# Order of loads on the GpSimd queue, the rows of the last two groups over three queues, and early tables for the second spectral layer

## The chip, the cores and the metric

The kernel runs on one core of one Trainium2 chip. The time of a run is the device time of one execution in microseconds; the time of a kernel is the median of its runs. The core has five instruction queues that work side by side and wait for each other through semaphores: PE (matrix multiplication), DVE (vector), ACT (scalar and activation functions), POOL (GpSimd) and SP (here it only issues transfers). Each works its instructions in the order in which they were written. Transfers are issued from SP, ACT and POOL.

## What is computed

Four layers, one after the other, on x of 2048 rows and 1024 columns in bfloat16. A is a spectral layer, B a dense one:

```python
def _A_ref(x, w_r, w_i):
    X = rfft2(x.astype(float32))
    X = X * (w_r + 1j * w_i)
    return irfft2(X, s=(S, D)).astype(bfloat16)

def _B_ref(x, w1, b1, w2):
    h = einsum("bsd,df->bsf", x, w1) + b1
    sp = log1p(exp(-abs(h))) + where(h > 0, h, 0)
    return einsum("bsf,fd->bsd", h * tanh(sp), w2)

x = x + _A_ref(_layernorm(x), w_r, w_i)
x = x + _B_ref(_layernorm(x), w1, b1, w2)
x = x + _A_ref(_layernorm(x), w_r, w_i)
x = x + _B_ref(_layernorm(x), w1, b1, w2)
```

D is 1024, S is 2048 and F, the width of h, is 3584.

## The kernel before

A small planner in Python writes the program. Each buffer has a record of who wrote and read it last; an instruction that is added to a queue gets the waits that this record asks for, and stands in its queue at the place where the Python code adds it. So the order of the code is the order of each queue. x stays in SBUF all the time as 16 tiles of 128 rows (XS).

**Spectral layer** (`layer_A`, called with li 0 and 1). The transform over 2048 rows and 1024 columns is done as matrix products with tables of sines and cosines. It has these parts:

- `first_scales` (li 0 alone) finds the mean and the scale of each row on DVE and ACT. `scaled(j)` (L540) then multiplies the table M0 with the scale of the rows of one column: eight products of 128 x 128 for each j, on DVE (L549) and ACT (L546). So the scale comes in through the table, and x needn't be normalized itself. For li 1 the dense layer has written normalized rows, and the plain table M is used.
- `s1` (L552) multiplies XR, which holds x with its rows turned, with these tables: 16 groups j of eight matmuls (L564). Group j is copied out of PSUM by DVE if j is even (L572) and by ACT if it is odd (L570). For li 0, `scaled(0)` to `scaled(3)` come first, and `scaled(j + 4)` follows group j.
- Then come 12 steps (L775) in which eight groups g of frequencies are worked through, each at several stages at once: `s2` of group step (L625), `filter_bins` of the same group (li 0 alone: the filter's reversed half by matmuls on PE, L818, and copies on POOL, L826 and L829), `s3` of group step - 1 (L663 to L666, then the product with the filter on DVE, L674 to L681), `i1` of group step - 3 (L692), `i2` of group step - 4 (L713 and L731) in two halves, each copied to the buffer U by DVE (L739) or ACT (L741). `u_turn` then turns U's rows into UT, the input of the last transform.
- `u_turn(g, half)` (L743): the eight rows of the first half go to UT one by one, each a transfer of 32 KB issued by SP. The second half of groups 0 to 6 goes with one store to DRAM (u_scratch, by SP) and one read back into UT, issued by POOL, which waits for the store. The last group's 16 rows go one by one over SP, POOL and ACT.
- At the end of a step POOL issues what later steps need: `load_tabs` (the table FT for s3), `load_w` (the filter: the raw w_r and w_i for li 0, which filter_bins works up, and for li 1 the worked-up filter that the dense layer has kept in DRAM, w_scratch), `load_btabs` (the table BT for i1). The first ones are issued ahead of s1 (L759 to L763). FT and BT have three buffers each, U three.
- `constants` (L390, li 0 alone, called between those first loads and s1): SP loads four tables and the bias of the dense layer, and POOL casts the bias to float32 (L399).

All transfers go through one helper, so they carry the line L242 (the bias L241); the line of an instruction that issues one doesn't tell which it is, the names of what it writes and reads do.

**Dense layer** (`layer_B`, called after each spectral layer). `i4` (L859, L865) does the last transform from UT and adds to x; it needs all of UT. Then x is normalized, transposed (L896) and multiplied with W1 (`mm1`, L914) and W2 (`mm2`, L932). W1 is streamed by SP through four buffers, whose first four loads are issued at the end of layer_A (L797 to L799); W2's 28 loads follow on SP. In the first dense layer, `keep_filter` (L835) works up the filter for the second spectral layer with its own reversal table (JT2), raw filter and work buffers, and stores it to w_scratch. Tiles of x that are finished are normalized at once and stored by SP; POOL reads them back turned into XR (`xr_load`, after `open_xr`). The last of them, tile 15, goes straight from SBUF to XR in eight rows, issued by SP and ACT in turn (`xr_direct`, L492).

The buffers WT of the second layer's filter lie where W1's four buffers are.

Of the kernel before, what the change touches and what calls it, by code (L numbers as in the profile page):

```python
# [6 lines left out]
ALU = mybir.AluOpType  # L7
P = 128
# [166 lines left out]
class KB:  # L175
# [364 lines left out]
    def scaled(self, j):  # L540
        rt = self.RT
        rc = rt.ap.rearrange("p a b -> p (a b)")
        for q in range(8):
            n = 8 * j + q
            if q % 3 == 2:
                self.op(self.act, lambda e, n=n: e.activation(self.MN.ap[:, n, :], self.M0.ap, ACT.Copy, scale=rc[:, n:n + 1]),  # L546
                        reads=[rt.res, self.M0.res], parts=[self.r_mn[j]])
            else:
                self.op(self.dve, lambda e, n=n: e.tensor_scalar(self.MN.ap[:, n, :], self.M0.ap, rc[:, n:n + 1], None, op0=ALU.mult),  # L549
                        reads=[rt.res, self.M0.res], parts=[self.r_mn[j]])  # L550

    def s1(self, li):  # L552
# [22 lines left out]
        for r in ([self.MN.res, self.M0.res] + self.r_xr if not li else []):  # L575
            r.r(self.pe, self.pe.count)
            self.XR.res.r(self.pe, self.pe.count)

    def layer_A(self, li):
# [3 lines left out]
        K = 1024  # L583
        o = self.o
        pe, dve, act, sp, pool = self.pe, self.dve, self.act, self.sp, self.pool
        ring = lambda name, n, size, shape: [self.alloc(f"{name}{i}", o[name] + size * i, shape) for i in range(n)]
        WT = ring("WT", 8, 2 * K, [2, 512])
        FT = ring("FT", 3, 1536, [2, 384])
        BT = ring("BT", 3, 1536, [2, 384])
        if li == 0:  # L590
            WR = ring("WR", 2, 4 * K, [2, 2, 512])
        FD, BD = self.FD, self.BD
        SIG = 2.0 / (self.S * self.D)

        def load_tabs(g):
            self.dma(pool, FT[g % 3].ap, self.con["FT"][g], f"ft{g % 3}", writes=[FT[g % 3].res])

        def load_btabs(g):
            self.dma(pool, BT[g % 3].ap, self.con["BT"][g], f"bt{g % 3}", writes=[BT[g % 3].res])

        def load_w(g):
            if li == 0:
                self.load_wr(WR[g % 2], g)
                return
            pair = WT[2 * g % 8:2 * g % 8 + 2]
            ap = self.ARENA[:, (o["WT"] + 2 * g % 8 * 2 * K) // 2:(o["WT"] + 2 * g % 8 * 2 * K) // 2 + 2 * K]
            self.dma(pool, ap.rearrange("p (a b c) -> p a b c", a=2, b=2), self.w_d[g], f"wt{g % 4}", reads=[self.r_wd[g]],
                     writes=[w.res for w in pair])

        def filter_bins(g):  # L610
            ps, banks, _ = self.pair()
            self.filter_bins(g, ps, banks, WR[g % 2], WT[2 * g % 8:2 * g % 8 + 2], self.JT, self.r_jt, pool)

        def zslot(g, i):
            return Z[(2 * g + i) % 6]
# [85 lines left out]
        def i2(g, half):  # L701
# [38 lines left out]
            else:  # L740
                self.op(act, lambda e: e.activation(dst, ps, ACT.Copy), reads=banks, parts=[u.res])  # L741

        def u_turn(g, half):  # L743
# [20 lines left out]
        if li == 0:  # L764
# [70 lines left out]
    def keep_filter(self, g):  # L835

        o = self.o
        if g == 0:
            jt = self.alloc("JT2", o["JT2"], [4 * P])
            self.dma(self.pool, jt.ap, self.con["JT"], "jt2", writes=[jt.res])  # L840
            self.kf = (jt, self.alloc("WR2", o["WR2"], [2, 2, 512]),
                       [self.alloc(f"WS{i}", o["WT2"] + 2048 * i, [2, 512]) for i in range(2)])
            self.load_wr(self.kf[1], 0)
        jt, wr, ws = self.kf
        self.filter_bins(g, self.PS[:, 6:8, :].rearrange("p a b -> p (a b)"), self.r_bank[6:8], wr, ws, jt.ap, jt.res, self.dve)
        ap = self.ARENA[:, o["WT2"] // 2:o["WT2"] // 2 + 2048].rearrange("p (a b c) -> p a b c", a=2, b=2)
# [21 lines left out]
            self.op(self.act, lambda e: e.activation(dst, src, ACT.Copy), reads=rb, parts=[staged.res])  # L868


    def load_w1(self):
        n = self.w1_next
        self.w1_next += 1
        fg = n % 14
        b = self.w1_buf[n % 4]
        self.dma(self.sp, b.ap, self.w1.rearrange("(db dp) f -> dp db f", dp=P)[:, :, fg * 256:(fg + 1) * 256], f"w1_{n % 4}",
                 writes=[b.res])

    def layer_B(self, li, last):
        pe, dve, act, sp, pool = self.pe, self.dve, self.act, self.sp, self.pool  # L880
# [107 lines left out]
        for c in range(2):  # L988
            off = self.ob[f"AT{c}"]
# [92 lines left out]
```

## Time and profile before

| | |
|---|---|
| median of 3 runs | 1183.19 us (1181.63 to 1184.5) |
| profiled execution | 1183.94 us |
| span of its instructions | 1182.1 us |
| mean granted clock of TensorE | 0.938 |
| busy: PE, DVE, ACT, POOL | 1000.5, 383.3, 335.4, 112.7 us |

Stages of the profiled execution, from the chain of waits in order of time: the first spectral layer from the start to 182.87 us, where the first `i4` begins; the dense layer to 617.3; the second spectral layer to 758.75; the second dense layer to the end.

How to read it: a group's row has the line, the engine, the operation, what it writes and reads, the number of instructions, busy time and mean duration, then the idle time before them and what ended it. A row of a timeline has start and duration, then the same; a number in brackets is how long the engine had been idle, and what it waited for. In the names, c_ft and c_bt are the tables FT and BT in DRAM, in_A_w_r and in_A_w_i the raw filter, ARENA is the part of SBUF in which most buffers lie, so that ARENA<-ARENA as a transfer is a row of U on its way to UT, or a row of tile 15 on its way to XR. SPq, ACTq and POOLq are the queues in which transfers are issued.

### The profile page before, as it was taken

How to read it: one execution, taken by the hardware profiler on the slowest of the kernel's cores; microseconds unless marked ns; L12 is line 12 of the kernel's file. 1: busy time of each engine (PE TensorE's matmuls, PEld its weight loads, DVE VectorE, ACT ScalarE, POOL GpSimd, SP SyncE). 2: the span in 40 equal slices, each digit the busy share in tenths (PEclk: the TensorE clock that was granted, in tenths of full speed). 3: DMA queues.
4: the chain of work that ended last, by engine and by line, in shares of the span. 5: the costliest groups of instructions: out<-in, count | busy, mean ns of one | idle time of the engine just before them, and what ended most of it. 6: DMA issues, size and time to landing. Idle time of an engine off the chain costs nothing.

```text
span 1182.1 us, 14518 instructions
## 1 busy us (share of the span) xinstructions
PE 1000.5 (85%) x6090; PEld 529.5 (45%) x6185; DVE 383.3 (32%) x843; ACT 335.4 (28%) x466; POOL 112.7 (10%) x155
## 2 busy tenths in 40 slices
PE   1776725999999999999985775279999999999998
PEld 0555514444444444444434543244444444444443
DVE  7796406360143501104344841264301210000111
ACT  6645513434100044420004744143330002442000
POOL 1254210000000012100330111100000000000000
PEclk9988865999999999999997977689999999999999
DMA  9624473254300045400683354804451001220000
GB/s 279 134 81 118 94 116 81 72 161 143 107 27 19 21 130 180 143 1 19 86 124 86 109 122 87 142 2 143 143 161 35 19 26 46 72 72 1 27 18 27
DMA packets 128735, 102.49 MB, mean 87 GB/s; under 512 B 48192, under 2 KB 105792, under 8 KB 128672
## 3 DMA queue, kind: packets, MB, share of 16 engines
q1 hardware_dynamic: 114976, 69.86, 21.9%
q0 software_dynamic: 11392, 31.19, 11.6%
q10 hardware_dynamic: 2304, 0.53, 0.4%
q8 instruction: 49, 0.80, 0.3%
q14 instruction: 14, 0.11, 0.0%
HBM read 80.45 MB, written 15.99 MB: 82 GB/s over the span
## 4 chain that ended last, share of the span: by engine, by line
PE 68%; DVE 13%; DMA 10%; ACT 2%; issue 2%; SPq 2%; POOL 2%; ACTq 0%; POOLq 0%; DVEq 0%
PE PS L932 33%; PE PS L914 28%; DMA ARENA<-in_A_w_i_dram 3%; DMA u_scratch<-ARENA 2%; DMA ARENA<-ARENA 2%; DVE BN L431 2%; SPq L242 2%; DMA ARENA<-c_bt 1%; POOL ARENA L242 1%; DVE ARENA L572 1%; PE PS L896 1%; DVE ARENA L549 1%; PE PS L818 1%; DVE XS L865 1%; PE PS L692 1%
## 5 line engine op out<-in xcount | busy, mean ns | idle before, releaser
L914 PE MATMUL PS<-ARENA 128*128 128x512 bf16 x1750 | 388.4, 381 | 4.4 <-DVE ARENA L901 2.2
L932 PE MATMUL PS<-ARENA 128*128 128x512 bf16 x1754 | 387.4, 379 | 2.0
L918 ACT ACTIVATE ARENA<-PS,B 128x512 bf16<-128x512 f32 x224 | 153.6, 687 | 436.5 <-PE PS L914 436.5
L914 PEld LDWEIGHTS PS<-ARENA 128*128 128x128 bf16 x1792 | 175.3, 98 | 211.1 <-issue 3.3
L932 PEld LDWEIGHTS PS<-ARENA 128*128 128x128 bf16 x1792 | 174.7, 98 | 207.7
L937 DVE TENSOR_TENSOR XS<-PS,XS 128x512 bf16<-128x512 f32 x64 | 44.3, 692 | 500.6 <-PE PS L932 500.6
L431 DVE BATCH_NORM_STATS2 BN<-XS 128x6 f32<-128x512 bf16 x108 | 69.6, 674 | 7.4 <-DMA XS<-in_A_x_dram 6.2
L859 PE MATMUL PS<-MT,ARENA 128*128 128x32 bf16 (+1 forms) x768 | 24.4, 188 | 52.5 <-DMA ARENA<-ARENA 44.2
L865 DVE TENSOR_TENSOR XS<-PS,XS 128x512 bf16<-128x512 f32 (+1 forms) x40 | 29.1, 790 | 101.2 <-PE PS L859 101.2
L692 PE MATMUL PS<-ARENA 128*128 128x256 bf16 x256 | 38.9, 302 | 22.1 <-DMA ARENA<-c_bt 21.0
L570 ACT ACTIVATE ARENA<-PS 128x1024 bf16<-128x1024 f32 x16 | 16.2, 1022 | 120.6 <-PE PS L564 120.1
L859 PEld LDWEIGHTS PS<-MT,ARENA 128*128 128x128 bf16 x768 | 22.8, 101 | 56.0 <-issue 48.9
L670 ACT ACTIVATE ARENA<-PS 128x1024 bf16<-128x1024 f32 x32 | 32.7, 1023 | 46.0 <-PE PS L666 46.0
L692 PEld LDWEIGHTS PS<-ARENA 128*128 128x128 bf16 x256 | 27.1, 108 | 35.2 <-issue 21.0
L699 ACT ACTIVATE ARENA<-PS 128x1024 bf16<-128x1024 f32 x32 | 32.7, 1021 | 30.0 <-PE PS L692 30.0
L674 DVE TENSOR_TENSOR ARENA<-ARENA 128x1024 bf16<-128x1024 bf16 x32 | 24.5, 766 | 46.7 <-ACT ARENA L670 46.5
L412 ACT ACTIVATE ARENA<-XS 128x1024 bf16<-128x1024 bf16 x20 | 21.1, 1056 | 64.5 <-DVE XS L865 53.5
L625 PE MATMUL PS<-FD,ARENA 128*128 128x256 bf16 (+1 forms) x312 | 36.9, 273 | 2.6 <-DVE ARENA L572 2.4
L818 PE MATMUL PS<-ARENA 128*128 128x64 bf16 x192 | 24.8, 293 | 11.8 <-DMA ARENA<-in_A_w_i_dram 8.9
L713 PE MATMUL PS<-ARENA,BD 128*128 128x256 bf16 x192 | 30.9, 307 | 3.0 <-DVE ARENA L739 2.6
L625 PEld LDWEIGHTS PS<-FD,ARENA 128*128 128x128 bf16 x312 | 28.6, 106 | 9.7 <-DVE ARENA L572 2.9
L896 PE MATMUL PS<-IDENT,ARENA 128*128 128x128 bf16 x256 | 23.1, 252 | 9.5 <-DVE ARENA L474 7.8
(71 smaller groups left out, 622.9 us busy)
## 6 DMA issues: line engine op xcount, KB each, us to landing
ARENA<-in_B_w_dram SPq DMA_DIRECT2D x56, 512.0 KB, 3.9
ARENA<-in_B_w_dram SPq DMA_DIRECT2D x56, 256.0 KB, 4.2
XS<-in_A_x_dram SPq DMA_DIRECT2D x4, 1024.0 KB, 8.7
ARENA<-in_A_x_dram SPq DMA_DIRECT2D x32, 128.0 KB, 3.1
ARENA<-in_A_w_r_dram POOLq DMA_DIRECT2D x16, 256.0 KB, 4.2
ARENA<-in_A_w_i_dram POOLq DMA_DIRECT2D x16, 256.0 KB, 4.6
ARENA<-ARENA SPq DMA_DIRECT2D x128, 32.0 KB, 3.2
w_scratch<-ARENA POOLq DMA_DIRECT2D x8, 512.0 KB, 3.0
```

The lines of the kernel that those rows point to most:

```text
L242: return eng.dma_start(out_ap, in_ap).then_inc(ds.sem, 16)
L431: self.op(self.dve, lambda e: e.bn_stats(self.BN[:, j, 6 * h:6 * h + 6], self.XS[:, j, 512 * h:512 * h + 512]), reads=[self.r_xs[j]], part ...
L625: fns.append(lambda e: e.matmul(dst, at(r), FD[:, t:t + dst.shape[-1] * 2], start=start, stop=stop))
L692: fns.append(lambda e, c=c, part=part: e.matmul(ps[:, c * 256:(c + 1) * 256], yk.ap[:, part, c * P:(c + 1) * P], t[:, (128, 0)[part]:(384, ...
L818: fns.append(lambda e, col=col, j=(j0 + c) * P, mov=mov: e.matmul(ps[:, col:col + 64], jt[:, j:j + P], mov, start=True, stop=True))
L859: fns.append(lambda e, l=l: e.matmul(ps[:, w * l:w * l + w], self.UT.ap[:, u0 + l, :], self.MT[:, 8 * lo:8 * lo + w], start=True, stop=True))
L865: self.op(self.dve, lambda e: e.tensor_tensor(xs, src, xs, ALU.add), reads=rb, parts=self.r_xs[lo:lo + nb])
L896: fns.append(lambda e, db=db: e.transpose(PSb[:, bank, db * P:(db + 1) * P], xn.ap[:, db * P:(db + 1) * P], self.IDENT[:]))
L914: fns.append(lambda e, db=db, bank=bank, fl=fl: e.matmul(PS[:, bank, :], wb.ap[:, db, fl * P:(fl + 1) * P], x.ap[:, db, :], start=(db == 0 ...
L918: self.op(act, lambda e, bank=bank, ft=ft: e.activation(at.ap[:, ft, :], PS[:, bank, :], ACT.Mish, bias=self.B1[:, ft:ft + 1]), reads=[sel ...
L932: fns.append(lambda e, i=i, ft=ft: e.matmul(PS[:, bank, :], at.ap[:, ft, t * P:(t + 1) * P], W2[ft].ap[:, h * 512:(h + 1) * 512], start=(i ...
L937: self.op(dve, lambda e: e.tensor_tensor(xs, PS[:, bank, :], xs, ALU.add), reads=[self.r_bank[bank]], writes=[self.r_xs[j]])
```

## The change

`xr_direct` issues its eight rows from SP, ACT and POOL in turn. In `scaled`, of each eight products ACT takes the second and the sixth (before: the third and the sixth), POOL the third, fifth and eighth, and DVE the other three (before: six).

The first loads of a spectral layer move into a function `open_tables`. For li 0 it is called where the loads were before, ahead of `constants` and `s1`. For li 1 it is called in the first dense layer, after the `mm2` of the third quarter of the rows and ahead of the `xr_load`s.

Within the steps, the read back of a group's second half is no longer issued in `u_turn` but at the end of the next step, behind the loads of that step (`u_back`). Only groups 0 to 5 still go through DRAM. Group 6 goes row by row: its first half from SP, its second from POOL. Group 7's first half goes from SP and POOL by turns, its second from ACT (five rows) and SP (three).

W1's first four loads and the load of the reversal table JT2 now wait until UT has been written.

```diff
-            prog = self.act if h % 2 else self.sp
+            prog = (self.sp, self.act, self.pool)[h % 3]
...
-            if q % 3 == 2:
+            if q % 4 == 1:
                 self.op(self.act, lambda e, n=n: e.activation(...))
             else:
-                self.op(self.dve, lambda e, n=n: e.tensor_scalar(...))
+                self.op(self.pool if q % 8 in (2, 4, 7) else self.dve, lambda e, n=n: e.tensor_scalar(...))
...
+    def open_tables(self, li):
+        self.li = li
+        self.WT = self.ring("WT", 8, 2048, [2, 512])
+        self.FTr = self.ring("FT", 3, 1536, [2, 384])
+        self.BTr = self.ring("BT", 3, 1536, [2, 384])
+        if li == 0:
+            self.WR = self.ring("WR", 2, 4096, [2, 2, 512])
+        for g in range(2 if li == 0 else 4):
+            self.load_w(g)
+        for g in range(2):
+            self.load_tabs(g)
+            self.load_btabs(g)
...
     def layer_A(self, li):
         if li == 0:
             self.junk = self.alloc("JUNK", self.o["JUNK"], [self.D])
             self.first_scales()
         if li == 0:
+            self.open_tables(0)
+            self.constants()
...
-            if half and g < 7:
+            if half and g < 6:
                 self.dma(sp, self.u_d[g], u.ap[:, 8:16, :], f"uw{g % 3}", reads=[u.res], writes=[self.r_ud[g]])
-                self.dma(pool, self.UT.ap[64 + g:P:8, :, :], self.u_d[g].rearrange("l r n -> r l n"), f"um{g % 3}",
-                         reads=[self.r_ud[g]], parts=[self.UT.res])
                 return
+            order = {6: (sp, pool), 7: ((sp, pool, sp, pool, sp, pool, sp, pool), (act, sp, act, act, sp, act, sp, act))}
+            who = order[g][half] if g in order else sp
             for i in range(8):
-                r = 8 * half + i
-                prog = sp
-                if g == 7:
-                    prog = (sp, sp, pool, sp)[i % 4] if half == 0 else (act, act, pool, act)[i % 4]
-                self.dma(prog, self.UT.ap[r * 8 + g:r * 8 + g + 1, :, :], u.ap[:, r, :], f"u{prog.name}{g % 3}",
-                         reads=[u.res], parts=[self.UT.res])
-
-        for g in range(2 if li == 0 else 4):
-            load_w(g)
-        for g in range(2):
-            load_tabs(g)
-            load_btabs(g)
-        if li == 0:
-            self.constants()
+                row(who[i] if isinstance(who, tuple) else who, g, 8 * half + i)
+
+        def u_back(g):
+            self.dma(pool, self.UT.ap[64 + g:P:8, :, :], self.u_d[g].rearrange("l r n -> r l n"), f"um{g % 3}",
+                     reads=[self.r_ud[g]], parts=[self.UT.res])
         self.s1(li)
...
             if 0 <= g4 < 8 and g4 + 2 < 8:
                 load_btabs(g4 + 2)
+            if 0 <= g5 - 1 < 6:
+                u_back(g5 - 1)
...
-            self.load_w1()
+            self.load_w1(after=[self.UT.res])
...
-            self.dma(self.pool, jt.ap, self.con["JT"], "jt2", writes=[jt.res])
+            self.dma(self.pool, jt.ap, self.con["JT"], "jt2", reads=[self.UT.res], writes=[jt.res])
...
         if not last:
             self.open_xr()
+            self.open_tables(1)
             for j in range(12):
                 self.xr_load(j)
```

More of the change, by code (lines that the diff above doesn't have):

```diff
@@ L548, in scaled @@
             else:
[L549 removed]
+                self.op(self.pool if q % 8 in (2, 4, 7) else self.dve, lambda e, n=n: e.tensor_scalar(self.MN.ap[:, n, :], self.M0.ap, rc[:, n:n + 1], None, op0=ALU.mult),
                         reads=[rt.res, self.M0.res], parts=[self.r_mn[j]])
@@ L577, in s1, with ring, load_tabs, load_btabs @@
             self.XR.res.r(self.pe, self.pe.count)
+    def ring(self, name, n, size, shape):
+        return [self.alloc(f"{name}{i}", self.o[name] + size * i, shape) for i in range(n)]
+    def open_tables(self, li):
[10 more added lines that the diff above has]
+            self.load_btabs(g)
+    def load_tabs(self, g):
+        b = self.FTr[g % 3]
+        self.dma(self.pool, b.ap, self.con["FT"][g], f"ft{g % 3}", writes=[b.res])
+    def load_btabs(self, g):
+        b = self.BTr[g % 3]
+        self.dma(self.pool, b.ap, self.con["BT"][g], f"bt{g % 3}", writes=[b.res])
+    def load_w(self, g):
+        if self.li == 0:
+            self.load_wr(self.WR[g % 2], g)
+            return
+        i = 2 * g % 8
+        off = (self.o["WT"] + 2048 * i) // 2
+        ap = self.ARENA[:, off:off + 2048].rearrange("p (a b c) -> p a b c", a=2, b=2)
+        self.dma(self.pool, ap, self.w_d[g], f"wt{g % 4}", reads=[self.r_wd[g]], writes=[w.res for w in self.WT[i:i + 2]])
     def layer_A(self, li):
@@ L582, in layer_A @@
             self.first_scales()
[L583 to L589, printed above, removed]
-        if li == 0:
-            WR = ring("WR", 2, 4 * K, [2, 2, 512])
+        if li == 0:
+            self.open_tables(0)
+            self.constants()
+        o, K = self.o, 1024
+        dve, act, sp, pool = self.dve, self.act, self.sp, self.pool
+        ring, load_tabs, load_btabs, load_w = self.ring, self.load_tabs, self.load_btabs, self.load_w
+        WT, FT, BT = self.WT, self.FTr, self.BTr
         FD, BD = self.FD, self.BD
         SIG = 2.0 / (self.S * self.D)
[L595 to L601, printed above, removed]
-            if li == 0:
[L603 to L608, printed above, removed]
         def filter_bins(g):
             ps, banks, _ = self.pair()
-            self.filter_bins(g, ps, banks, WR[g % 2], WT[2 * g % 8:2 * g % 8 + 2], self.JT, self.r_jt, pool)
+            self.filter_bins(g, ps, banks, self.WR[g % 2], WT[2 * g % 8:2 * g % 8 + 2], self.JT, self.r_jt, pool)
         def zslot(g, i):
@@ L868, in i4, with load_w1 @@
             self.op(self.act, lambda e: e.activation(dst, src, ACT.Copy), reads=rb, parts=[staged.res])
-    def load_w1(self):
+    def load_w1(self, after=()):
         n = self.w1_next
@@ L876, in load_w1 @@
         self.dma(self.sp, b.ap, self.w1.rearrange("(db dp) f -> dp db f", dp=P)[:, :, fg * 256:(fg + 1) * 256], f"w1_{n % 4}",
-                 writes=[b.res])
+                 reads=after, writes=[b.res])
     def layer_B(self, li, last):
```

5 lines of the change are left out of this document (4 added, 1 removed).

## The prediction

> **What bounds the kernel now.** I read the page's summary of the chain that ended last, then that chain in order of time through both spectral layers, then the timelines of POOL, PE and SP there.
>
> ```profile
> PE 68%; DVE 13%; DMA 10%; ACT 2%; issue 2%; SPq 2%; POOL 2%; ACTq 0%; POOLq 0%; DVEq 0%
> ```
>
> PE carries the dense layers; the 10% of DMA is the place to look. In order of time (start, duration, what) the first spectral layer has:
>
> ```profile
> 47.83 2.27 DVE ARENA L572 x2
> ...
> 93.77 2.39 DMA u_scratch<-ARENA
> ...
> 96.45 2.37 POOL ARENA L242 x3
> 98.81 7.51 DMA ARENA<-in_A_w_i_dram
> ...
> 164.17 5.53 DMA u_scratch<-ARENA
> ...
> 169.99 2.76 POOL ARENA L242 x4
> 172.75 9.71 DMA ARENA<-ARENA
> ...
> 182.87 1.03 PE PS L859 x32
> ```
>
> The first row is the end of s1, at 50.1. The middle three are the pattern: a store of turned rows to DRAM lands, POOL, which waited for it, issues the read back, and only then the filter load that was queued behind it; PE stands still for that. The last four are the tail: store, read back, four last rows from POOL, 9.71 us to landing, and the inverse transform starts at 182.87. The second layer shows the same in PE's timeline (in brackets the idle time before and what ended it):
>
> ```profile
> 662.22 0.39 PE L663 MATMUL PS<-ARENA 128*128 128x512 bf16 x1
> ...
> 669.65 0.38 PE L663 MATMUL PS<-ARENA 128*128 128x512 bf16 x1
> ...
> 681.65 0.58 PE L663 MATMUL PS<-ARENA 128*128 128x512 bf16 x1 [4.64 <-DMA ARENA<-c_ft]
> ...
> 705.18 0.59 PE L663 MATMUL PS<-ARENA 128*128 128x512 bf16 x1 [5.02 <-DMA ARENA<-c_ft]
> ...
> 758.75 3.42 PE L859 MATMUL PS<-MT,ARENA 128*128 128x32 bf16 x122 [23.24 <-DMA ARENA<-ARENA]
> ```
>
> Steps 4, 5, 6 and 8 begin at the first four rows. Undisturbed, a step takes 669.65 - 662.22 = 7.4 us; PE then waits for tables, and at the end 23 us for rows.
>
> **Part 1: the scaled copies of the first table, three of eight on POOL.** DVE's 96 multiplies become 48, and POOL gets 48. POOL works its queue in order, and ahead of them stands the cast of the bias: constants() is called before s1. Today:
>
> ```profile
> 49.26 0.21 POOL L399 CAST B<-B1h 128x28 f32<-128x28 bf16 x1 [29.61 <-DMA B1h<-in_B_b_dram]
> 49.41 0.85 POOL L826 COPY ARENA<-ARENA 128x384 bf16<-128x384 bf16 x1
> 50.21 0.63 POOL L829 COPY ARENA<-ARENA 128x256 bf16<-128x256 bf16 x1
> 50.78 0.85 POOL L826 COPY ARENA<-ARENA 128x384 bf16<-128x384 bf16 x1
> ```
>
> ```profile
> 7.01 32.34 SPq L242 DMA_DIRECT2D ARENA<-in_A_x_dram  x32
> ```
>
> ```profile
> 25.34 4.00 DVE L549 TENSOR_SCALAR ARENA<-ARENA 128x128 bf16<-128x128 bf16 x24
> ```
>
> The bias is issued on SP behind those 32 loads of x, which the change leaves alone, and has landed at 49.26; the cast that waits for it delays nobody today. After the change each of the 16 matmul groups of s1 needs three columns from POOL, so the first can't start before about 50, where s1 now ends. PE's s1 waits for that, then the whole layer. The price of the multiply on POOL isn't in the trace: copies start 0.80 us apart for 384 columns and 0.57 for 256, which makes 0.34 for 128. From 49.41, 48 x 0.34 = 16.3 gives 65.7; a last copy (1.02, row below) and a matmul group ahead of it, put at the same, end at 67.7 instead of 50.1: **+17.6 us**. From below, at DVE's price of 4.00 / 24 = 0.17, POOL would be through at 57.6, but then ACT is last: held at its first copy until about 52, it has 8 copies and 22 of its own multiplies left:
>
> ```profile
> 25.34 3.03 ACT L546 ACTIVATE ARENA<-ARENA 128x128 bf16<-128x128 bf16 x10 [4.49 <-DVE ARENA L532]
> 28.52 1.02 ACT L570 ACTIVATE ARENA<-PS 128x1024 bf16<-128x1024 f32 x1
> ```
>
> 8 x 1.02 + 22 x 0.30 = 14.8, so 66.8 and +16.7: with the cast where it stands there is no gain. From above, 0.57 a multiply and DVE in the way, it is +34.5 (a rival below). I take 0.34, because the cast of 28 columns, 0.15 to the next start, lies on the line through the copies too.
>
> **Part 2: table and filter loads ahead of the read back, first layer.** The loads of a step now wait for their buffers alone, which are free by then; the read back comes a step late, when its store (2.39 us) has landed. PE's timeline:
>
> ```profile
> 81.23 1.55 PE L818 MATMUL PS<-ARENA 128*128 128x64 bf16 x12 [2.67 <-DVE ARENA L655]
> ...
> 91.27 1.55 PE L818 MATMUL PS<-ARENA 128*128 128x64 bf16 x12
> ...
> 106.37 1.55 PE L818 MATMUL PS<-ARENA 128*128 128x64 bf16 x12 [6.34 <-DMA ARENA<-in_A_w_i_dram]
> ...
> 120.46 1.55 PE L818 MATMUL PS<-ARENA 128*128 128x64 bf16 x12
> ...
> 132.09 0.63 PE L664 MATMUL PS<-ARENA 128*128 128x512 bf16 x1 [3.85 <-DMA ARENA<-c_ft]
> ```
>
> These are the filters of steps 4 to 7 and the start of step 8. Leaving part 1's shift aside: filter 6 at 106.37 - 6.34 = 100.0; filter 7 one undisturbed step later (91.27 - 81.23 = 10.0) at 110.0; step 8 after what lies between without its wait, 132.09 - 3.85 - 120.46 = 7.8, at 117.8. What is late next is SP, which issues rows one by one:
>
> ```profile
> 710.56 1.23 DVE L739 CAST ARENA<-PS 128x1024 bf16<-128x1024 f32 x1 [0.34 <-PE PS L713]
> ```
>
> ```profile
> 88.67 5.06 SPq L242 DMA_DIRECT2D ARENA<-ARENA  x8
> ```
>
> ```profile
> ARENA<-in_B_w_dram SPq DMA_DIRECT2D x56, 512.0 KB, 3.9
> ...
> ARENA<-ARENA SPq DMA_DIRECT2D x128, 32.0 KB, 3.2
> ```
>
> In the second layer group 4's rows are ready 711.8 - 705.2 = 6.6 us into step 8; 1.4 of that I take off, because PE's matmuls there take 0.59 instead of 0.38 after the wait: 5.2. From then SP has 9 + 9 + 8 + 7 = 33 issues for groups 4 to 7, at 5.06 / 8 = 0.63 each, 20.8, and 3.2 to landing; PE follows 0.4 later (182.87 against 172.75 + 9.71). That is 29.6 from the start of step 8, so the inverse transform starts at 147.4 instead of 182.87: **-35.5 us**. POOL fits beside it with twelve rows and two read backs at no more than 2.76 / 4 = 0.7 each, 10 us; so do ACT's five rows.
>
> **Part 3: the same in the second layer.** Step 6 at 681.65 - 4.64 = 677.0, step 8 at 677.0 + 2 x 7.4 = 691.8, the inverse transform at 691.8 + 29.6 = 721.4 instead of 758.75: **-37.4 us**.
>
> **Part 4: the second layer's tables early, the last normalized tile over three queues.**
>
> ```profile
> 520.62 4.75 PE PS L932 x22
> ...
> 621.16 0.51 ACTq L242
> ...
> 623.24 8.04 DMA ARENA<-ARENA
> ```
>
> ```profile
> 569.47 7.43 POOL L242 DMA_DIRECT2D ARENA<-xn_scratch  x7 [74.37 <-PE PS L932]
> ...
> 615.05 2.19 POOL L242 DMA_DIRECT2D ARENA<-w_scratch  x4
> ```
>
> The buffers of four of these loads are W1's, read until the second half of the dense layer takes over at 520.62; POOL idles until 569.47, so the eight loads fit there, hidden by PE's 50 us. Today they are issued from 615.05 on and share the DMA engines with the tile's eight rows, whose last takes 8.04 us to land against the usual 3.2: **-4.8 us**, or nothing if the loads were late after all. The third queue saves one issue of four, within this rounding.
>
> **What costs nothing.** W1's first loads now wait for the turned rows, and W2's are queued behind them on SP. PE's first dense matmul comes 18 us after the first inverse one (201.03 below against 182.87), and a load of W1 lands 3.9 us after its issue; if that cover were gone, each microsecond would cost one. The reversal table of the dense layer waits for the turned rows on POOL; behind it stand only loads that wait until 248.04 today.
>
> ```profile
> 201.03 9.17 PE L914 MATMUL PS<-ARENA 128*128 128x512 bf16 x31 [1.19 <-DVE ARENA L901]
> ```
>
> ```profile
> 248.04 0.73 POOL L242 DMA_DIRECT2D ARENA<-in_A_w_r_dram  x1 [74.22 <-DVE XS L865]
> ```
>
> **Sum.** 17.6 - 35.5 - 37.4 - 4.8 = -60.1 on the profiled execution's 1183.94 (1.84 over its span) gives 1123.8. The median of the runs is 0.75 lower, 1183.19, so I say 1123. This case's own range is 1113 to 1134: 2 us either way in part 1, 4 each in parts 2 and 3 for steps less regular than the two I measured them by.
>
> **Rivals.** *The tails stay long* (0.12). Today's last rows took 9.71 us to land, not 3.2, and W1's loads, which now wait, ran beside them; if the rows themselves were the cause, each layer gives 6.5 back: 1136.
>
> *POOL's multiply is dear, and DVE blocks it* (0.09). At 0.57 each, and 0.16 more for each of the 36 multiplies that DVE has left after its first twelve, POOL takes 27.4 + 5.8 = 33.2 and the stage costs 34.5: 1140. For it: one DVE instruction takes 0.69 alone and 3.24 while POOL is busy.
>
> ```profile
> 90.52 0.69 DVE L676 TENSOR_TENSOR ARENA<-ARENA 128x1024 bf16<-128x1024 bf16 x1
> ...
> 111.38 3.24 DVE L676 TENSOR_TENSOR ARENA<-ARENA 128x1024 bf16<-128x1024 bf16 x1
> ```
>
> Against it: DVE's multiplies are 6 us of a stage of 18, and POOL's first copy above, begun at 49.41 beside DVE's last one from 47.83 to 50.1, took no longer than its third. The Trainium skill's page "SBUF — State Buffer", section "Who interferes with whom", calls it an exclusive lock on a shared port pair, in which whichever of DVE and GpSimd comes second fully blocks. The two rows agree that the engines hold each other up; no row shows it for this pair of operations. By that rule alone, with 0.34 a multiply, the 5.8 us would be added to the sum: 1129.
>
> *The cast doesn't hold POOL* (0.06). Then POOL starts at 25.3 and s1 is held by x alone, issued until 39.4; ending near 47 it gives 3 instead of costing 17.6: 1103.
>
> *Slower* (0.03). POOL's multiply by a per-partition scalar is far dearer than its copy. Parts 2 to 4 give 77.7 and the stage costs 1.3 + 48t, so this decides from t = 1.6 us on; at 1.8 the time is 1194. POOL takes 0.85 for three times the columns, so I hold it unlikely.
>
> **How the numbers follow.** Forecast 0.70, rivals 0.12, 0.09, 0.06 and 0.03. The range 1110 to 1146 takes in the forecast's own and the first two rivals, with some room above 1140 because POOL's price is bounded only by neighbours; it leaves out the last two, 0.09. A change within 0.2% (2.4 us; about what a measurement of this kernel can tell from no change) needs t close to 1.6: same 0.01, slower 0.03, faster 0.96.
>
> **What would show it.** Right: POOL's first multiply right after the cast near 49.3, the first matmul of s2 near 68, no wait of PE for a filter or a table after step 4, the inverse transform 97 us after s1 ends (133 today), W1's loads after the last row. Wrong: multiplies before 49; their starts over 0.5 us apart; rows landing over 5 us after their issue; steps of over 11 us in the first layer or 8 in the second with every table there.

## The result, and the profile after

The changed kernel takes 1155.09 us, the median of four runs (1152.63 to 1155.79), against 1183.22 for the kernel before beside it (1181.63 to 1184.5): a ratio of 0.9759, 95% interval 0.974 to 0.9778. It is faster by 28 us. The forecast was 60, and 1155 lies 9 us above the range's upper end.

The profiled execution has a span of 1152.8 us, 29.3 less than before. By stages (`s2` is the first L642 matmul, L625 before; `i4` the first L875, L859 before; the second layer is counted from its first L564):

| stretch | before | after | change | forecast |
|---|---|---|---|---|
| start to first `s2` | 50.15 | 80.72 | +30.6 | +17.6 |
| first `s2` to first `i4` | 132.72 | 104.81 | -27.9 | -35.5 |
| first `i4` to the last `mm2` of that dense layer | 434.46 | 436.1 | +1.6 | 0 |
| wait for the last turned rows of x | 14.3 | 13.1 | -1.2 | -4.8 |
| second layer's `s1` to `i4` | 127.12 | 95.55 | -31.6 | -37.4 |
| from there to the end | 423.35 | 422.5 | -0.8 | 0 |
| sum | | | -29.3 | -60.1 |

Three lines of the page: the chain's summary, and two groups of PE (busy time, mean ns, then idle time before and what ended it).

```profile
PE 70%; DVE 9%; DMA 8%; issue 5%; POOL 4%; ACT 3%; SPq 1%; ACTq 0%; POOLq 0%; DVEq 0%
...
L564 PE MATMUL PS<-ARENA 128*128 128x128 bf16 x128 | 16.2, 306 | 38.4 <-POOL ARENA L549 33.5
L709 PE MATMUL PS<-ARENA 128*128 128x256 bf16 x256 | 34.1, 277 | 2.3 <-DMA ARENA<-c_bt 2.3
```

DMA's share fell from 10% to 8%, POOL's rose from 2% to 4%. The second row says why: in the first `s1` PE now waits 33.5 us for POOL's multiplies. The third shows one of the waits that were to go, for the tables of `i1`: 2.3 us are left in the whole run.

The chain in order of time (start, duration, what), its pieces in both spectral layers:

```profile
50.52 27.90 POOL ARENA L549 x47
78.55 1.01 PE PS L564 x8
79.56 1.16 issue
80.72 1.87 PE PS L642 x8
...
166.82 8.67 DMA u_scratch<-ARENA
175.77 2.71 POOL ARENA L242 x4
178.48 6.48 DMA ARENA<-ARENA
185.53 1.03 PE PS L875 x32
...
690.45 6.16 DMA u_scratch<-ARENA
696.89 1.10 POOL ARENA L242
698.00 7.13 DMA ARENA<-c_bt
705.27 1.03 PE PS L709 x8
...
712.11 8.99 DMA u_scratch<-ARENA
721.51 2.19 POOL ARENA L242 x3
724.21 5.63 DMA ARENA<-ARENA
730.30 1.03 PE PS L875 x32
```

The pattern "store, read back, and then a load" in the middle of the first layer is gone. In the second layer it stands once more, at 690.45: the table BT of the last group is issued behind the read back of group 2, which waited for its store, and this is the 2.3 us of the third line above. Otherwise the two tails are left, of the same form as before: store (5.53 and 6.48 us before, now 8.67 and 8.99), POOL, last rows, `i4`. And at 50.52 there is a new piece, 27.9 us of POOL alone.

POOL's timeline, around that piece and at the second layer's early loads:

```profile
49.64 0.21 POOL L399 CAST B<-B1h 128x28 f32<-128x28 bf16 x1 [29.91 <-DMA B1h<-in_B_b_dram]
49.91 2.37 POOL L549 TENSOR_SCALAR ARENA<-ARENA 128x128 bf16<-128x128 bf16 x4
...
504.51 0.55 POOL L242 DMA_DIRECT2D ARENA<-w_scratch  x1 [6.79 <-PE PS L930]
...
527.41 0.54 POOL L242 DMA_DIRECT2D ARENA<-c_bt  x1
```

The cast holds POOL until 49.64, and the multiplies stand behind it, as forecast. Their price is not: 47 in 27.90 us are 0.594 each. The second row is cut at 52 us; DVE's next instruction begins at 52.89, so these four were made with DVE idle, at 2.37 / 4 = 0.59.

### The profile page after: what moved, and what is told of

It is laid out like the page before. It is cut to its first block, busy times and chain, and to the rows that moved or that the text cites. A ratio compares the mean times of both kernels' runs of the same rounds, so it can differ in the third digit from the quotient of the medians.

```text
span 1152.8 us, 14555 instructions
## 1 busy us (share of the span) xinstructions
PE 986.0 (86%) x6090; PEld 522.3 (45%) x6185; DVE 377.2 (33%) x795; ACT 335.1 (29%) x466; POOL 149.0 (13%) x219
## 4 chain that ended last, share of the span: by engine, by line
PE 70%; DVE 9%; DMA 8%; issue 5%; POOL 4%; ACT 3%; SPq 1%; ACTq 0%; POOLq 0%; DVEq 0%
PE PS L948 33%; PE PS L930 28%; DMA ARENA<-in_A_w_i_dram 3%; POOL ARENA L549 2%; DMA u_scratch<-ARENA 2%; DMA ARENA<-ARENA 2%; POOL ARENA L242 1%; PE PS L642 1%; DVE BN L431 1%; PE PS L912 1%; DVE XS L881 1%; PE PS L834 1%; DMA XS<-in_A_x_dram 1%; PE PS L709 1%; PE PS L730 1%
## 5 line engine op out<-in xcount | busy, mean ns | idle before, releaser
L930 PEld LDWEIGHTS PS<-ARENA 128*128 128x128 bf16 x1792 | 175.5, 98 | 213.0 <-issue 4.5
L948 PEld LDWEIGHTS PS<-ARENA 128*128 128x128 bf16 x1792 | 174.7, 98 | 207.6
L875 PE MATMUL PS<-MT,ARENA 128*128 128x32 bf16 (+1 forms) x768 | 24.5, 187 | 47.9 <-DMA ARENA<-ARENA 39.6
L564 PE MATMUL PS<-ARENA 128*128 128x128 bf16 x128 | 16.2, 306 | 38.4 <-POOL ARENA L549 33.5
L875 PEld LDWEIGHTS PS<-MT,ARENA 128*128 128x128 bf16 x768 | 22.9, 100 | 51.4 <-issue 44.7
L642 PE MATMUL PS<-FD,ARENA 128*128 128x256 bf16 (+1 forms) x312 | 35.5, 266 | 2.7 <-DVE ARENA L572 1.2
L709 PE MATMUL PS<-ARENA 128*128 128x256 bf16 x256 | 34.1, 277 | 2.3 <-DMA ARENA<-c_bt 2.3
L242 POOL DMA_DIRECT2D w_scratch<-ARENA x8 | 4.6, 576 | 230.9 <-ACT ARENA L848 230.9
L572 DVE CAST ARENA<-PS 128x1024 bf16<-128x1024 f32 x16 | 19.1, 1222 | 45.4 <-PE PS L564 45.4
L642 PEld LDWEIGHTS PS<-FD,ARENA 128*128 128x128 bf16 x312 | 27.6, 103 | 9.3 <-issue 1.9
L564 PEld LDWEIGHTS PS<-ARENA 128*128 128x128 bf16 x128 | 12.4, 138 | 42.2 <-issue 39.1
```

The costliest lines, as they stand in the source:

```text
L564: fns.append(lambda e, q=q, n=n, ps=ps, m=m: e.matmul(ps[:, q * P:(q + 1) * P], XR.ap[:, n, :], m, start=True, stop=True))
L642: fns.append(lambda e: e.matmul(dst, at(r), FD[:, t:t + dst.shape[-1] * 2], start=start, stop=stop))
L709: fns.append(lambda e, c=c, part=part: e.matmul(ps[:, c * 256:(c + 1) * 256], yk.ap[:, part, c * P:(c + 1) * P], t[:, (128, 0)[part]:(384, ...
L875: fns.append(lambda e, l=l: e.matmul(ps[:, w * l:w * l + w], self.UT.ap[:, u0 + l, :], self.MT[:, 8 * lo:8 * lo + w], start=True, stop=True))
L930: fns.append(lambda e, db=db, bank=bank, fl=fl: e.matmul(PS[:, bank, :], wb.ap[:, db, fl * P:(fl + 1) * P], x.ap[:, db, :], start=(db == 0 ...
L948: fns.append(lambda e, i=i, ft=ft: e.matmul(PS[:, bank, :], at.ap[:, ft, t * P:(t + 1) * P], W2[ft].ap[:, h * 512:(h + 1) * 512], start=(i ...
```

## The experiments

Each kernel was timed beside the kernel before (medians of 1184.88, 1182.43 and 1184.8 in three sets; the first holds e1 to e4, the second e5 to e8, the third the rest). This table has the stages of their profiled executions: the first `s2`, and then the length of the two stretches that the forecast spoke of.

| kernel | time | ratio, 95% interval | first `s2` at | `s2` to `i4` | second `s1` to `i4` |
|---|---|---|---|---|---|
| after | 1155.09 | 0.9759 (0.974 to 0.9778) | 80.72 | 104.81 | 95.55 |
| e1 | 1123.42 | 0.9487 (0.9466 to 0.9509) | 50.23 | 102.40 | 95.17 |
| e2 | 1128.1 | 0.9538 (0.951 to 0.9566) | 56.37 | 102.81 | 94.95 |
| e3 | 1215.16 | 1.0258 (1.0227 to 1.029) | 80.70 | 132.82 | 126.20 |
| e4 | 1155.8 | 0.9757 (0.9722 to 0.9792) | 80.30 | 107.20 | 94.99 |
| e5 | 1149.68 | 0.9718 (0.9689 to 0.9747) | 80.19 | 101.61 | 92.96 |
| e6 | 1152.92 | 0.9758 (0.9731 to 0.9784) | 80.42 | 103.49 | 94.61 |
| e7 | 1150.55 | 0.9739 (0.9708 to 0.977) | 79.81 | 104.73 | 95.25 |
| e8 | 1148.26 | 0.9711 (0.9683 to 0.9739) | 80.17 | 101.19 | 93.92 |
| e9 | 1122.38 | 0.9475 (0.9439 to 0.9511) | 50.07 | 103.51 | 95.98 |
| e10 | 1119.42 | 0.9461 (0.9436 to 0.9487) | 47.65 | 103.44 | 91.25 |
| e11 | 1129.86 | 0.9561 (0.9524 to 0.9599) | 50.30 | 103.90 | 100.93 |
| e12 | 1164.41 | 0.9834 (0.981 to 0.9858) | 80.51 | 109.84 | 101.59 |

### POOL's multiplies: e1, e2, e3

**e1**, the change without its new split of the multiplies:

```diff
-            if q % 4 == 1:
+            if q % 3 == 2:
...
-                self.op(self.pool if q % 8 in (2, 4, 7) else self.dve, lambda e, n=n: e.tensor_scalar(...))
+                self.op(self.dve, lambda e, n=n: e.tensor_scalar(...))
```

> The changed kernel with the scaled table's columns made by DVE and ACT alone, as before the change. Theory: POOL's 48 multiplies, 0.594 us each and behind the cast of the bias, cost the first stage 30.6 us (s2 starts at 80.72 instead of 50.15), and nothing later absorbs it: 1124.5, s2 at about 50. Rival: what the stage loses is partly hidden, since tables and filters have landed long before in the late start; then the time falls by 20 or less, to 1135 or more.

**e2**, the change with the cast of the bias behind `s1` on POOL's queue:

```diff
-        self.op(self.pool, lambda e: e.tensor_copy(self.B1[:], self.B1h[:]), reads=[r], writes=[self.r_b1])
+        self.r_b1h = r
...
         self.s1(li)
+        if li == 0:
+            self.op(self.pool, lambda e: e.tensor_copy(self.B1[:], self.B1h[:]), reads=[self.r_b1h], writes=[self.r_b1])
```

> The changed kernel with the cast of the bias on POOL moved behind s1; POOL still makes three of eight columns. Theory: the cast holds POOL from 25.3 to 49.9, and the price of 0.594 is the operation's own. So POOL works from 25.4 for 28.5 us, s2 starts near 56, 25 us earlier: 1130. Rival: the price comes from DVE working beside POOL, which it does much more from 25 us on; then POOL's multiplies take 0.7 or more and s2 starts at 61 or later: 1136 or more.

**e3**, the kernel before with the new split alone (e1's edit the other way round, on the kernel before):

> The kernel before with nothing changed but the split of the scaled table's columns over DVE, ACT and POOL. Theory: part 1 alone costs its 30.6 us: 1213.8. Rival: the kernel before waits for its loads on POOL anyway, and these have 30 us more to land; then it costs 20 or less: 1203.

e1's first `s2` is back at 50.23, and its time 31.7 below that of the change. e3 is 30.3 above the kernel before. So the split alone costs the 30.6 us of the table, and nothing else in the change touches that stage. Nothing later absorbs it: e3's two stretches are 132.82 and 126.20, against 132.72 and 127.12 in the kernel before. e2 parts the 30.6 in two: without the cast, `s2` begins at 56.37, so the cast accounts for 24.4 and POOL's price for the other 6.2. POOL's row in e2:

```profile
25.30 28.76 POOL L549 TENSOR_SCALAR ARENA<-ARENA 128x128 bf16<-128x128 bf16 x48 [5.76 <-DVE ARENA L532]
```

and DVE's rows in e2, beside it:

```profile
25.23 2.23 DVE L549 TENSOR_SCALAR ARENA<-ARENA 128x128 bf16<-128x128 bf16 x12
...
29.66 1.32 DVE L549 TENSOR_SCALAR ARENA<-ARENA 128x128 bf16<-128x128 bf16 x6
```

28.76 / 48 = 0.60 over a stretch in which DVE multiplies a good third of the time, against 0.59 with DVE idle. POOL's first four, made beside DVE's twelve, end at 27.91, 0.65 each. So DVE adds some 0.06 while it multiplies, and doesn't set POOL's price. DVE's own multiplies rose from 4.00 / 24 = 0.17 before to 2.23 / 12 = 0.19 and 1.32 / 6 = 0.22.

### Which part brings the gain: e11

The kernel before with one edit: the read back of a group's second half is issued one step later, behind that step's loads.

```diff
-                self.dma(pool, self.UT.ap[64 + g:P:8, :, :], self.u_d[g].rearrange("l r n -> r l n"), f"um{g % 3}",
-                         reads=[self.r_ud[g]], parts=[self.UT.res])
...
                 load_btabs(g4 + 2)
+            if 0 <= g5 - 1 < 7:
+                g = g5 - 1
+                self.dma(pool, self.UT.ap[64 + g:P:8, :, :], self.u_d[g].rearrange("l r n -> r l n"), f"um{g % 3}",
+                         reads=[self.r_ud[g]], parts=[self.UT.res])
```

> The kernel before with nothing changed but the place of the read backs on POOL: at the end of the next step, behind its table and filter loads (all seven groups still go through DRAM, the rows of group 7 stay on their old queues, W1's loads wait for nothing, the second layer's tables stay late). Theory: nearly all of the gain is this order, since neither the rows' queues nor W1's wait was worth a measurable time: 1184 less 55 to 60 is 1124 to 1129. Rival: the parts need each other, and late tables or W1's loads beside the rows take a good part back: 1135 or more.

It takes 1129.86, 54.9 below the kernel before. PE's timeline in e11, the starts of `s2`, the first `i4`, the second `s1` and the second `i4`:

```profile
50.30 1.89 PE L625 MATMUL PS<-FD,ARENA 128*128 128x256 bf16 x8 [1.23 <-DVE ARENA L572]
...
154.20 4.93 PE L861 MATMUL PS<-MT,ARENA 128*128 128x32 bf16 x179 [20.67 <-DMA ARENA<-u_scratch]
...
604.94 10.51 PE L564 MATMUL PS<-M,ARENA 128*128 128x128 bf16 x128 [15.16 <-DMA ARENA<-ARENA]
...
705.87 5.97 PE L861 MATMUL PS<-MT,ARENA 128*128 128x32 bf16 x224 [24.58 <-DMA ARENA<-u_scratch]
```

The stretches are 28.8 and 26.2 shorter than before; in the change they are 27.9 and 31.6 shorter. This order is the gain in the first layer, whole; in the second the rest of the change adds 5.4. Which part of the rest does, no run shows: e4 and e7 below each take one part back, and their second stretch stays at 95 us. Not all of the gain is waiting time. PE's own busy time falls from 80.89 to 74.31 us in the first stretch and from 75.71 to 68.84 in the second, with the matmuls unchanged: those right behind a long wait had taken longer, as the rows of 0.58 to 0.63 in the prediction show, against 0.38 or 0.39 elsewhere. The tails stay: PE still stands 20.67 and 24.58 us ahead of `i4`.

### The tails: e4, e12, e8, e7, e5

**e4**, the change with the rows of groups 6 and 7 as they were before:

```diff
-            if half and g < 6:
+            if half and g < 7:
...
-            order = {6: (sp, pool), 7: ((sp, pool, sp, pool, sp, pool, sp, pool), (act, sp, act, act, sp, act, sp, act))}
+            order = {7: ((sp, sp, pool, sp, sp, sp, pool, sp), (act, act, pool, act, act, act, pool, act))}
...
-            if 0 <= g5 - 1 < 6:
+            if 0 <= g5 - 1 < 7:
```

> The changed kernel with the rows of the last two groups as before: group 6's second half through DRAM, group 7's rows from SP, POOL and ACT in the old shares. Theory: SP has 33 issues for groups 4 to 7 either way, but the last read back now waits for group 6's store instead of group 5's, which is issued some 6 us later, so each spectral layer's tail is 4 to 8 us longer: 1163 to 1171. Rival: the tail is bound by the DMA engines (busy share over 1 from 168 to 182 us), which the direct rows of group 6 fill; then the old way costs nothing or wins: 1150 to 1156.

It takes 1155.8, as the change does. My theory, that the spread of the rows saves 8 us or more, is wrong: the ratios are 0.9757 and 0.9759, so the new spread is worth nothing that these runs can tell from noise.

**e12**, the other way: all rows of groups 6 and 7 from SP alone.

```diff
-            order = {6: (sp, pool), 7: ((sp, pool, sp, pool, sp, pool, sp, pool), (act, sp, act, act, sp, act, sp, act))}
-            who = order[g][half] if g in order else sp
+            who = sp
```

> The changed kernel with all rows of groups 6 and 7 issued by SP. Theory (rows of several queues at once hold each other up): with one queue a row lands in about 3 us to the end, so the longer issue, 50 instead of 33 at 0.63, 10.7 us more, is half made good by 4 us less to landing and no read back behind POOL's rows: each tail 3 to 6 us longer, 1161 to 1167. Rival: a row takes 6 us or more in the tail whatever the queue; then each tail is 9 to 11 us longer: 1173 or more.

It is 9 us slower than the change, but its rows land quickly. The DMA view by issue (count, size, median us from issue to landing; the first row is the DMA engines' busy share in 40 slices, in tenths), e12 from 160 to 195 us:

```profile
DMA  7952222878632147865323113113122120006999
...
ARENA<-ARENA SPq DMA_DIRECT2D x40, 32.0 KB, 2.8
u_scratch<-ARENA SPq DMA_DIRECT2D x2, 256.0 KB, 4.2
```

The change, from 167 to 186 us:

```profile
DMA  8995999999999999999998799899899521000000
...
ARENA<-ARENA SPq DMA_DIRECT2D x15, 32.0 KB, 7.4
ARENA<-ARENA POOLq DMA_DIRECT2D x11, 32.0 KB, 6.8
u_scratch<-ARENA SPq DMA_DIRECT2D x1, 256.0 KB, 8.7
ARENA<-u_scratch POOLq DMA_DIRECT2D x1, 256.0 KB, 8.1
ARENA<-ARENA ACTq DMA_DIRECT2D x4, 32.0 KB, 8.4
```

With one queue the engines are well below full in most slices, and a row lands in 2.8 us: SP issues its 50 transfers with hardly a break from 153.88 to 188.08, and this is the bound. With three queues they are full in most slices and these transfers take 6.8 to 8.7 us: the engines are most of the bound. The rows are issued sooner and land later; what is left of the saving is 5.0 us in the first layer and 6.0 in the second. The Trainium skill's page "DMA: Bandwidth & Descriptors", section "Issuing engines are not separate DMA queues", has the rule: transfers from several engines run on the same 16 DMA engines, so a second issuer saves issue time alone. These two rows agree. It adds that issue time is usually small beside the transfer. In e12 it isn't: one row's 0.63 us is small beside its landing of 2.8, but 50 issues one after the other set the end.

**e8** leaves out group 6's eight rows on POOL, so that part of UT isn't written for that group; it asks whether less traffic lets the rest land sooner.

```diff
+            if g == 6 and half:
+                return
             who = order[g][half] if g in order else sp
```

> The changed kernel without the eight rows of group 6's second half from POOL: they are left out, so that part of UT is stale. Theory (rows from several queues at once fill the DMA engines): the store of group 5, which takes 8.67 us to land, lands in 5 or less, and each tail is 4 us shorter or more: 1147 or less. Rival (the store is late because SP issues it late and works its own rows off in order): it still takes 7 us or more, and the time falls by less than 4: 1151 to 1155.

At 1148.26 it lies between the two theories. The store of group 5, on which they turned, took 7.0 us to land in the first tail and 3.6 in the second: one for the rival, one for the theory. From 160 to 182 us:

```profile
ARENA<-ARENA SPq DMA_DIRECT2D x24, 32.0 KB, 3.7
...
ARENA<-ARENA ACTq DMA_DIRECT2D x5, 32.0 KB, 4.7
ARENA<-ARENA POOLq DMA_DIRECT2D x4, 32.0 KB, 4.5
```

and from 702 to 724:

```profile
ARENA<-ARENA SPq DMA_DIRECT2D x20, 32.0 KB, 6.1
ARENA<-u_scratch POOLq DMA_DIRECT2D x2, 256.0 KB, 9.7
```

In the first layer the rows land in about half the time, as contention among them would have it (from 167 on, as in the change's view above, SP's 15 rows take 3.9, against 7.4). In the second they don't: 6.1, against 6.2 in the change from 710 to 731. There PE had waited 5.33 us for a table just before, and two read backs were issued close together, at 706.84 and 708.77, beside the rows. So the number of rows may be part of it, and is not the whole.

**e7**, W1's first loads not held back:

```diff
-            self.load_w1(after=[self.UT.res])
+            self.load_w1()
```

> The changed kernel with W1's first loads not waiting for the turned rows, as before the change. Theory: they take DMA time from the last rows, and each tail is about 4 us longer: 1163. Rival: the last rows are slow by themselves, and W1's loads behind SP's last row come too late to matter: 1155.

My theory of 1163 is wrong: 1150.55, a ratio whose interval overlaps that of the change. In its first tail W1's loads are issued from 176.94 on, beside the last rows; from 165 to 186 us:

```profile
ARENA<-in_B_w_dram SPq DMA_DIRECT2D x4, 512.0 KB, 8.0
ARENA<-ARENA SPq DMA_DIRECT2D x16, 32.0 KB, 6.3
```

The rows land in 6.3 us, no later than without (7.2 in the same window of the change), and both stretches are as long as in the change. Holding W1 back neither costs nor brings anything that these runs can tell from noise. In the kernel before W1's loads began 4 us ahead of POOL's last rows; what part of its 9.71 us was theirs wasn't tried.

**e5**, the read back of group 5, whose store is late in the chain above, behind group 7's rows on POOL instead of ahead of them:

```diff
-            if 0 <= g5 - 1 < 6:
+            if 0 <= g5 - 1 < 5:
                 u_back(g5 - 1)
+        u_back(5)
```

> The changed kernel with the read back of group 5 issued on POOL behind POOL's four rows of group 7 instead of ahead of them. These rows are ready at about 168 and stand behind a wait until 175.8. Theory (the DMA engines are full with the rows of three queues): the end is then set by the read back itself, issued at 175.8 and some 6 us to land, so each tail is 2 to 4 us shorter: 1147 to 1151. Rival (POOL's order sets the end): without the wait in front, the rows land by 176 and the read back in 3 us: each tail 5 us shorter or more, 1145 or less.

1149.68, a ratio of 0.9718; both stretches are some 3 us shorter (3.2 and 2.6). POOL's wait for the store has left the chain of the first tail, which now ends with SP's issues until 176.32 and 5.39 to landing. The interval just reaches that of the change, so this gain is likely and not sure.

### The second layer's start, and combinations: e6, e9, e10

**e6**, the third FT table of the second layer loaded early as well, so that no table load runs beside tile 15's rows:

```diff
             self.load_btabs(g)
+        if li:
+            self.load_tabs(2)
...
-            if 0 <= g3 < 8 and g3 + 2 < 8:
+            if (1 if li else 0) <= g3 < 8 and g3 + 2 < 8:
```

> The changed kernel with the third table FT of the second spectral layer loaded with the first two, during the dense layer, instead of right behind POOL's two rows of tile 15. Theory: that load, issued at 626.89, runs beside the last rows and holds the last of them up: with it gone the rows land in 3 to 4 us instead of 7.5, and the second layer starts 3 to 4 us earlier: 1151 to 1152. Rival: eight rows of one tile at once from three queues hold each other up, whatever else runs: no change, 1154 to 1156.

PE's wait for those rows went from 13.13 to 12.33, the ratio is that of the change. The tile's rows still take 5.7 to 6.8 us to land (median by queue), so the table load isn't what makes them slow. That they hold each other up fits, but no run took some of them away.

**e9** is e1 and e5 together.

> The changed kernel with two edits that were run singly: the scaled columns by DVE and ACT alone (1123.4) and the read back of group 5 behind POOL's last rows (some 5 us less than the changed kernel). Theory: they lie in different stages and add up: 1118. Rival: with an earlier stage the read back is on time anyway: 1123.

It can't be told from e1 (0.9475 against 0.9487), and neither stretch is shorter (103.51 and 95.98 against 102.40 and 95.17). e5's gain didn't come again: in the second tail the read back, though last on POOL, waited 4.13 us for its store, where in e5 it hadn't waited.

**e10** has POOL do two of eight multiplies, the cast late, and the edits of e5 and e6:

```diff
-                self.op(self.pool if q % 8 in (2, 4, 7) else self.dve, lambda e, n=n: e.tensor_scalar(...))
+                self.op(self.pool if q % 8 in (3, 7) else self.dve, lambda e, n=n: e.tensor_scalar(...))
```

> The changed kernel with POOL making two of eight scaled columns (the fourth and the eighth) instead of three, the cast of the bias behind s1, the read back of group 5 behind POOL's last rows, and the third table FT early. Theory: with 0.6 a multiply POOL needs 1.2 us for each group of s1, DVE with four multiplies and half a copy about 1.4, so the stage ends 22 to 23 us after 25.3, s2 starts at 48, 2 us earlier than with DVE and ACT alone: 1115. Rival: DVE's multiplies beside POOL's are as much dearer as they are fewer (0.20 to 0.26 instead of 0.16), so POOL's help is worth nothing: 1118 or more.

1119.42, the lowest median of all. POOL's share now fits beside DVE's: its row in e10

```profile
25.27 20.06 POOL L549 TENSOR_SCALAR ARENA<-ARENA 128x128 bf16<-128x128 bf16 x32 [5.80 <-DVE ARENA L532]
```

ends at 45.3, and `s2` begins at 47.65, 2.6 before e1's. That part is shown by the trace. The second stretch, 91.25, is 4.3 shorter than in the change, so what e5 brought there came again here, though not in e9. For the whole kernel the intervals of e10 and e1 overlap (up to 0.9487, from 0.9466).

## Why the prediction was right and wrong

The profiled execution fell 29.3 us and not 60.1. Of the 30.8 that are missing, 13.0 lie in the first stage, nearly all of it the price of POOL's multiply, 13.0 in the two tails and 3.6 in the wait for tile 15's rows; the rest is made up of small differences.

**Part 1, +17.6 forecast, +30.6 measured.** The mechanism was right: the cast of the bias holds POOL, the multiplies begin at 49.91, and all 16 groups of `s1` wait. The step that failed is "I take 0.34", the price of POOL's multiply from a line through two sizes of copy. It is 0.594; 48 times the difference, 12.2, is nearly the whole of the 13.0 missing. The upper bound of 0.57 was the better guide, and even that was too low. The rival "POOL's multiply is dear, and DVE blocks it" had the size of the stage nearly right (+34.5) with half of its cause: the price alone does it. The Trainium skill's page "SBUF — State Buffer", section "Who interferes with whom", states the lock, for a DVE instruction with one tensor as its input, for the two-port modes, which it says `tensor_scalar` can enter. Whether DVE's multiplies did, no run shows. If each of the twelve in e2 had blocked POOL for its 0.16, POOL's first four would have been 1.9 us later; they were 0.2 later (0.65 each against 0.59). DVE's own became 0.02 to 0.05 longer.

**Parts 2 and 3, the steps: right.** PE's timeline in the change has the start of step 8 in both layers (the first matmul of it in the first layer, 0.22 ahead, is missing from the records) and the one wait for a table that is left in the second:

```profile
150.07 0.38 PE L681 MATMUL PS<-ARENA 128*128 128x512 bf16 x1 [0.16 <-issue]
...
693.75 0.39 PE L680 MATMUL PS<-ARENA 128*128 128x512 bf16 x1
...
705.27 1.03 PE L709 MATMUL PS<-ARENA 128*128 128x256 bf16 x8 [2.29 <-DMA ARENA<-c_bt]
```

From the first `s2` to step 8 are 69.1 us; forecast were 117.8 - 50.15 = 67.7. In the second layer 59.0 us from `s1`; forecast 691.8 less 631.63, where `s1` stood before, 60.2. The waits for filters and tables went as argued, but for the 2.29 us of the last row (a table still behind a read back), and e11 shows that the order on POOL's queue did it. What is left of these waits cost little: e1 and e7 don't have this one, and PE stands 20.64 and 20.68 us ahead of their second `i4`, against 2.29 and 19.02 in the change.

**Parts 2 and 3, the tails: wrong.** Forecast were 29.6 us from step 8 to `i4`; they took 35.7 and 36.6. SP's timeline in the first layer:

```profile
155.23 5.88 SPq L242 DMA_DIRECT2D ARENA<-ARENA  x8
161.15 0.59 SPq L242 DMA_DIRECT2D u_scratch<-ARENA  x1
161.79 4.99 SPq L242 DMA_DIRECT2D ARENA<-ARENA  x8
166.82 0.64 SPq L242 DMA_DIRECT2D u_scratch<-ARENA  x1
167.51 10.59 SPq L242 DMA_DIRECT2D ARENA<-ARENA  x15
185.25 7.22 SPq L242 DMA_DIRECT2D ARENA<-in_B_w_dram  x5
```

Group 4's rows come 155.23 - 149.85 = 5.4 into the step (forecast 5.2). The 33 issues end at 178.10, 22.9 later (20.8). The last row is POOL's, issued 0.4 later because its read back waited for the store (8.67), and lands after 6.48 where I had "3.2 to landing"; PE follows 0.6 later. So 3.3 of the 6.1 are the landing, 2.1 the issues. The failed step is "3.2 to landing": 3.2 was the median of all rows, most of which went out from SP with little beside them, like these in the change from 121 to 150 us:

```profile
ARENA<-ARENA SPq DMA_DIRECT2D x29, 32.0 KB, 3.0
```

"POOL fits beside it" failed too, by less: its last rows stood behind a read back that waited for a store. e5, which takes that wait off the rows, is some 3 us shorter in each tail, a gain that isn't sure.

The rival "the tails stay long" had the right effect and the right size, 6.5 a layer. I had kept it small because W1's loads ran beside the 9.71 us before; in the change the last rows took 6.48 and 5.63 without W1's loads beside them, in e7's first tail 6.69 with them. Both rivals came true in size, and together: 1123 + 13.0 + 6.1 + 6.9 = 1149, and the next two points bring the rest. I had given each a chance by itself and never worked out their sum, and it was what went past the range.

**Part 4: wrong by 3.6.** The early loads came without cost, from 504.51 on (three of the four filter loads waited for W1's buffers one by one, from there to 525.23, about where the forecast put them). But tile 15's rows did not land in the usual 3.2, the step that failed here: e6 shows them at 5.7 to 6.8 with no table load beside them.

**What was to cost nothing** cost 1.6 us in the first dense layer, 1.4 of it in one wait of PE for ACT at 209.87. It is no cost that can be told from noise: the wait isn't there in e4 and e7, and over e1 to e12 the same stretch lasts from 433.8 (e5, e12) to 437.3 (e4). W1's loads cost nothing that e7 shows. The wait of the reversal table's load wasn't tried by itself; behind it, as argued, POOL's next instruction waits until 250.67 in any case.

**Open.** Why rows land in half the time in e8's first tail and not in its second; whether the read back behind the rows (e5, e9, e10) is worth anything; which part of the change besides the order brings 5.4 us in the second layer; what sets POOL's price of 0.59 for 128 columns, where its copy of 384 took 0.80 from start to start.

## What to carry to other kernels

In an in-order queue, look first at what stands ahead of the moved work: read backs that waited for their stores, ahead of loads that waited for nothing any more, cost this kernel 55 us over two layers, and one cast that waited for a late load made 24 of the 30 us that the new split lost. Take an operation's price on an engine from that operation on that engine, and where the trace has none, run the sum at the upper bound too, together with the other rivals and not one by one. Take a landing time from rows that were issued in the same company: the same 32 KB row took 2.8 us from one queue and 7.4 beside two others.

## What the runs showed of the hardware that was not expected

- A multiply of 128 x 128 bf16 by a per-partition scalar takes DVE 0.17 us alone and 0.19 to 0.22 beside POOL. It takes POOL 0.59 with DVE idle and 0.65 while DVE multiplies beside it (0.60 to 0.63 over the whole stage in e2 and e10).
- Three queues that issue single-partition rows of 32 KB at once fill the DMA engines (nine tenths in most slices of the change's first tail), and what is in flight slows: a row from 3.0 us (from 121 to 150 us) to 7.4, a 256 KB store from 3.9 to 8.7.
